# Paired input tiles, the first stage of batch 1 held in SBUF, and one first-stage tile earlier, in a Fourier layer ahead of two feed-forward layers

## The chip, the cores and the metric

One core of one Trainium2 chip runs the whole program. Times are microseconds (us) on the device. The kernel before took 1247.51 us, the median of three runs (1246.95 to 1249.55). All profiles are of a single execution.

## The reference

The input x has two batches of 3008 positions with 256 channels. A Fourier layer is followed by two feed-forward layers:

```python
X = np.fft.rfft(x, axis=1)                       # along the 3008 positions
Yr = Xr @ w_r - Xi @ w_i + b_r                   # complex 256 x 256 product
Yi = Xr @ w_i + Xi @ w_r + b_i
Yr = np.sign(Yr) * np.maximum(np.abs(Yr) - 0.01, 0.0)    # Yi likewise
y = np.fft.irfft(Yr + 1j * Yi, n=3008, axis=1)
h = y @ w_in                                     # 256 -> 2048
u = (h * np.clip(h + 3.0, 0.0, 6.0) / 6.0) @ w_out       # 2048 -> 256
g = u @ w_gate                                   # 256 -> 1536
out = (g / (1.0 + np.exp(-g)) * (u @ w_val)) @ w_out2    # 1536 -> 256
```

Inputs are float32, except that the weights of the feed-forward layers arrive as 64-bit numbers, which the kernel itself turns into float32.

## The kernel before

**The transform in two stages.** 3008 is 47 x 64, and the transform is done as a Fourier transform of length 47 (first stage), then one of length 64 (second stage). The first stage is a product of a constant 96 x 96 matrix, `fwd1_sb`, with x laid out as 96 rows. Each batch is cut into 8 tiles of 96 x 1024 numbers (384 KB), so there are 16 *first-stage tiles*; tiles 0 to 7 are batch 1, tiles 8 to 15 batch 2. `pre(n)` is one of them: it issues the load of tile n + 3 on SyncE (SP), does two products of 512 columns (the profile counts two passes of TensorE for each float32 product, so 4 in a tile), has ScalarE copy the first half out of PSUM and VectorE the second, into a buffer `bs`, and the store of that buffer to the DRAM scratch `Bd` follows on ScalarE's DMA queue (L252). The buffers `bs` come from a ring of four (tag `bc`, `ring4`), which later serves `cs` too. x has four buffers, two for even and two for odd tiles.

The second stage needs the rows regrouped, so it reads `Bd` back. The 96 rows are 24 groups of 4 rows, and a *quad* is four groups, 16 rows: quad 0 rows 0 to 15, quad 1 rows 16 to 31, up to quad 5. `load_q` (L279) loads a quad's `z` tile, 512 KB, with a run of 1 KB for each row and position; it needs the first stage of the whole batch in DRAM. It also loads that quad's table `m`.

**One quad.** With two batches there are 12 quads in turn, p = 0 to 11. For each of them:
- `s2` (L287), the *second stage*: products of z with m, in two halves of 8 passes. Behind it ScalarE casts the result to a high part, VectorE takes the difference as the low part, and ScalarE writes sign-flipped copies of both, into tiles `xh` and `xl`.
- `ln`, the *complex product* with the 256 x 256 matrices (`linh`, `linl`: `lin` split into a high and a low part by GpSimd in `prepare`), by `mm3` (L113 to L115, three products of parts), in two halves; behind each half VectorE adds the bias and does the soft threshold.
- `ia` (L333), the *inverse* of the second stage, into `cs`, stored to `Cd`. Its last stage, `post`, comes per block of tokens ahead of the feed-forward layer.

**Weights.** `Convert.step()` is one *weight step*: it advances the conversion of the first feed-forward layer's weights (64 pieces of 128 x 256) by one piece. In a step VectorE has four instructions (shift L161, tail L165, sign L174, low L181), ScalarE two (scale L156, high L177), and SP one load of 256 KB. Steps are issued by the first-stage tiles above 8, by `ln`, and by the *units* of the feed-forward layer (one unit is one block of tokens with one of 16 slices of the hidden width).

**The order.** All is written out by hand, in one list `seq`, in which each engine finds its own instructions in order; nothing is moved by a scheduler. The list begins with tile 0, `prepare`, tiles 1 to 7, `load_q` of quad 0, tiles 8 to 10 and the second stage of quad 0. Then each turn p brings the first half of quad p's product, half of the inverse of quad p - 1, a first-stage tile, the second stage of quad p + 1, the second half of the product, another tile, and the rest of the inverse, with two tiles a turn until all 16 are used:

```python
seq = P[:1] + [prepare] + P[1:NT] + [lambda: load_q(0, 0)] + P[NT : NT + 3] + S(0)
rest = P[NT + 3 :]
for p in range(len(ORDER)):
    l, a = L(p), A(p - 1)
    some, rest = rest[:2], rest[2:]
    seq += [l[0], a[0]] + u + some[:1] + S(p + 1)[:1] + u + S(p + 1)[1:] + [l[1]] + u + some[1:] + [a[1]] + u
```

`S(p + 1)` begins with the load of quad p + 2. Before any of this, TensorE runs three *warm-up* products on a tile of zeros (L225). Each engine's DMA issues take their semaphores from a few that come round in turn, so an issue can wait for the earlier DMA that had the same one.

## Time and profile before

| | before |
|---|---|
| time, median of 3 (range) | 1247.51 us (1246.95 to 1249.55) |
| profiled execution: time, span of its trace | 1247.67 us, 1245.9 us |
| TensorE (PE) busy, share of the span | 1228.3 us, 99% |
| TensorE weight loads (PEld) | 1034.2 us, 83% |
| VectorE (DVE) | 809.8 us, 65% |
| ScalarE (ACT) | 679.7 us, 55% |
| GpSimd (POOL) | 6.3 us, 1% |
| HBM read, written | 132.75 MB, 39.06 MB |

The span is the stretch from the first to the last instruction in the trace; the time of the execution has 1.8 us more around it. The products of TensorE follow one another without gaps nearly everywhere: in 40 slices of 31 us the profile shows it at 70% in the first, 80% in the second and 90% or more from there on, all but the last. The same first slices have the DMA engines at 90% and 90%, then 70%, 60%, 30%, and the granted TensorE clock at 90% and 80% of full speed, and at 90% or more afterwards.

### The profile page before, as it was taken

To read this page: it belongs to the slowest core of one execution; us is meant where nothing else is said; L and a number is where in the kernel's file an instruction comes from. 1 tells how busy PE (TensorE), PEld (TensorE's weight loads), DVE (VectorE), ACT (ScalarE), POOL (GpSimd) and SP (SyncE) were. 2 spreads that over 40 slices of the span, in tenths; PEclk is the share of its full clock that TensorE was granted. 3 is DMA by queue.
4 is the path that set the end of the run, shared out by engine and by line. 5 is a ranking of instruction groups with operands and counts; after the bars stand their busy time and mean duration, and the time that the engine had idled before them with its cause. 6 is when DMAs were issued, how large, how long until landed. Compare 5 with 4: busy or idle time off the path is not lost.

```text
span 1245.9 us, 15942 instructions
## 1 busy us (share of the span) xinstructions
PE 1228.3 (99%) x5914; PEld 1034.2 (83%) x5914; DVE 809.8 (65%) x1424; ACT 679.7 (55%) x1216; POOL 6.3 (1%) x15
## 2 busy tenths in 40 slices
PE   7899999999999999999999999999999999999998
PEld 2799987888888888888899888888888888888997
DVE  2587665666666666666656577676676676676665
ACT  2455544555555555555555566656656555656554
POOL 2000000000000000000000000000000000000000
PEclk9899999999999999999999999999999999999999
DMA  9976323033122122132032244554644644544551
GB/s 305 279 258 191 102 77 105 28 100 103 64 91 93 59 70 93 64 100 91 39 105 91 72 175 170 203 182 152 220 158 170 235 153 152 216 157 168 203 186 72
DMA packets 50285, 172.84 MB, mean 139 GB/s; under 512 B 4752, under 2 KB 18160, under 8 KB 39456
## 3 DMA queue, kind: packets, MB, share of 16 engines
q1 hardware_dynamic: 41856, 158.55, 37.4%
q10 hardware_dynamic: 8128, 12.58, 2.8%
q8 instruction: 46, 0.75, 0.2%
q0 software_dynamic: 224, 0.69, 0.2%
q14 instruction: 31, 0.25, 0.1%
HBM read 132.75 MB, written 39.06 MB: 138 GB/s over the span
## 4 chain that ended last, share of the span: by engine, by line
PE 96%; DMA 2%; DVE 0%; ACT 0%; issue 0%; SPq 0%; ACTq 0%; DVEq 0%
PE acc L114 12%; PE acc L115 12%; PE acc L113 12%; PE ph L113 7%; PE ph L115 7%; PE ph L114 7%; PE P L662 5%; PE P L663 5%; PE P L664 5%; PE Tb L663 3%; PE Tb L662 3%; PE Tb L664 3%; PE p L419 3%; PE p L113 2%; PE p L115 2%; PE p L114 2%
## 5 line engine op out<-in xcount | busy, mean ns | idle before, releaser
L434 DVE SCALAR_TENSOR_TENSOR r<-r,ph 128x512 f32<-128x512 f32 (+1 forms) x192 | 129.7, 676 | 83.3 <-ACT r L433 82.8
L118 DVE TENSOR_TENSOR gl<-r,gh 128x512 fp32r<-128x512 f32 (+1 forms) x192 | 130.1, 678 | 82.4 <-ACT gh L452 81.0
L433 ACT ACTIVATE r<-ph,three 128x512 f32<-128x512 f32 (+1 forms) x192 | 130.2, 678 | 96.1 <-PE ph L115 80.6
L452 ACT CAST gh<-r 128x512 fp32r<-128x512 f32 (+1 forms) x192 | 117.3, 611 | 84.4 <-DVE r L434 82.7
L113 PE MATMUL ph<-xah,w1l 128*128 128x512 f32 (+1 forms) x384 | 152.1, 396 | 0.0
L113 PE MATMUL acc<-gh,w1l 128*128 128x512 f32 (+1 forms) x384 | 148.3, 386 | 1.5 <-ACT gh L452 1.5
L114 PE MATMUL acc<-gl,w1h 128*128 128x512 f32 (+1 forms) x384 | 148.2, 386 | 0.2 <-DVE gl L118 0.2
L115 PE MATMUL ph<-xah,w1h 128*128 128x512 f32 (+1 forms) x384 | 148.2, 386 | 0.0
L114 PE MATMUL ph<-xal,w1h 128*128 128x512 f32 (+1 forms) x384 | 148.1, 386 | 0.0
L115 PE MATMUL acc<-gh,w1h 128*128 128x512 f32 (+1 forms) x384 | 148.1, 386 | 0.0
L118 DVE TENSOR_TENSOR gl<-s,gh 128x512 fp32r<-128x512 f32 (+1 forms) x144 | 97.3, 676 | 49.8 <-ACT gh L686 49.7
L662 PE MATMUL P<-xo,slot 128*128 128x512 f32 (+1 forms) x288 | 111.3, 386 | 1.7 <-DVE g L732 0.8
L114 PE MATMUL acc<-gl,slot 128*128 128x512 f32 (+1 forms) x288 | 111.1, 386 | 0.3 <-DVE gl L118 0.2
L113 PE MATMUL acc<-gh,slot 128*128 128x512 f32 (+1 forms) x288 | 111.0, 385 | 0.0
L664 PE MATMUL P<-xo,slot 128*128 128x512 f32 (+1 forms) x288 | 110.9, 385 | 0.0
L115 PE MATMUL acc<-gh,slot 128*128 128x512 f32 (+1 forms) x288 | 110.9, 385 | 0.0
L663 PE MATMUL P<-xo,slot 128*128 128x512 f32 (+1 forms) x288 | 110.9, 385 | 0.0
L728 ACT ACTIVATE s<-g 128x512 f32<-128x512 f32 (+1 forms) x72 | 44.9, 623 | 93.7 <-DVE g L726 93.7
L686 ACT CAST gh<-s 128x512 fp32r<-128x512 f32 (+1 forms) x144 | 88.1, 612 | 1.5 <-DVE s L745 1.2
L113 PEld LDWEIGHTS acc<-gh,w1l 128*128 128x128 f32 x384 | 72.1, 188 | 15.4 <-ACT gh L452 1.9
L114 PEld LDWEIGHTS acc<-gl,w1h 128*128 128x128 f32 x384 | 72.1, 188 | 14.6 <-DVE gl L118 0.9
L115 PEld LDWEIGHTS ph<-xah,w1h 128*128 128x128 f32 x384 | 72.1, 188 | 14.0
(94 smaller groups left out, 2258.7 us busy)
## 6 DMA issues: line engine op xcount, KB each, us to landing
slot<-Wd SPq DMA_DIRECT2D x72, 1152.0 KB, 5.1
st<-in_w SPq DMA_DIRECT2D x68, 256.0 KB, 3.8
Wd<-slot SPq DMA_DIRECT2D x12, 1152.0 KB, 4.7
x<-in_x SPq DMA_DIRECT2D x16, 384.0 KB, 6.5
Bd<-bs ACTq DMA_DIRECT2D x16, 384.0 KB, 5.9
z<-Bd SPq DMA_DIRECT2D x12, 512.0 KB, 6.1
Cd<-cs ACTq DMA_DIRECT2D x12, 512.0 KB, 3.5
Xd<-x SPq DMA_DIRECT2D x20, 256.0 KB, 2.1
```

The costliest lines, as they stand in the source:

```text
L113: nc.tensor.matmul(o, wl, xh, start=start, stop=False)
L114: nc.tensor.matmul(o, wh, xl, start=False, stop=False)
L115: nc.tensor.matmul(o, wh, xh, start=False, stop=stop)
L118: nc.vector.tensor_tensor(out=o, in0=full, in1=hi.bitcast(F32), op=ALU.subtract)
L433: nc.scalar.activation(r[:, :n], p[:, :n], AF.Relu, bias=three)
L434: nc.vector.scalar_tensor_tensor(out=r[:, :n], in0=r[:, :n], scalar=6.0, in1=p[:, :n], op0=ALU.min, op1=ALU.mult)
L452: nc.scalar.copy(hi[:, :n], g[:, :n])
L662: nc.tensor.matmul(o, wl, x[:, 0, :n], start=start, stop=False, skip_group_check=not start)
L663: nc.tensor.matmul(o, wh, x[:, 1, :n], start=False, stop=False, skip_group_check=not start)
L664: nc.tensor.matmul(o, wh, x[:, 0, :n], start=False, stop=True, skip_group_check=not start)
L686: nc.scalar.copy(hi[:, :nb], t[:, :nb])
L728: nc.scalar.activation(s0[:, :n], h, AF.Silu)
```

## The change

**Input.** x lies in DRAM as pairs of tiles, *pair* k being tiles 2k and 2k + 1, with 8 KB for each of the 96 rows. There are four rooms of 128 partitions x 2048; rooms 2 and 3 use the space of the tiles `X` (the former `xh` and `xl`, now one tile). Pair 0 comes as two loads of 96 rows, in partitions 0 to 95. Each later pair comes as two loads, 64 rows into every second partition (0, 2, 4, ...), and 32 rows into every fourth (1, 5, 9, ...); the partitions that no row goes to are set to zero by memsets beforehand, of room 1 by VectorE, of rooms 2 and 3 and the end of room 0 by GpSimd. `fwd1_sb` is 128 x 192: the plain matrix, and one whose rows are spread in the same way. Four pairs are issued at the start and the others after tiles 4, 6, 9 and 11 (`REFILL`).

**First stage.** Batch 1's output goes into one SBUF tile, `stage1`, in space that later holds half of the first layer's weights. Its rows 0 to 31 (the *early rows*, those of quads 0 and 1) are stored by ScalarE after tiles 1, 3, 5, 6 and 7. The other 64 (the *held rows*) are stored by two DMAs of SP, issued behind the load of quad 1's z. Batch 2's output goes into buffers of two tiles, from a *ring of two*, stored once for each two tiles; `cs` uses the same ring, two quads to a buffer.

**Order.** `prepare` stands first, twelve first-stage tiles come ahead of the second stage of quad 0 instead of eleven, tile 12 directly behind it, and one tile follows in turn 0 and two in turn 1. There are two warm-up products instead of three. The first four tiles of batch 2 that had a weight step have none now; the step function is the same, and the steps not yet done are taken up by units 8 to 10 of the feed-forward layer. `inv2` is loaded by SP at turn 6 instead of by GpSimd at the start.

The diff (the parts that only follow a renamed tile are left out):

```diff
-    out = {"fwd1": fwd1, "inv2": fwd1.T, "fwd2": fwd2, "inv1": inv1}
+    both = np.zeros((128, 2 * GW))
+    both[:QP, :GW] = fwd1
+    both[::2, GW:], both[1::4, GW:] = fwd1[:64], fwd1[64:]
+    out = {"fwd1": both, "inv2": fwd1.T, "fwd2": fwd2, "inv1": inv1}
...
-    Bd = [dram.tile([GW, NJ * DIM], F32, name=f"Bd{b}") for b in range(NB)]
+    Bd = [dram.tile([n, NJ * DIM], F32, name=f"Bd{n}") for n in (32, GW - 32, GW)]
...
-    fwd1_sb = misc.tile([QP, GW], F32, name="fwd1_sb")
+    fwd1_sb = misc.tile([128, 2 * GW], F32, name="fwd1_sb")
...
-    def pieces(p, name, src, nf, n, into):
-        out = []
-        for f in range(nf):
-            t = [p.tile([128, n, 256], F32R, name=f"{name}{i}_{f}") for i in "hl"]
-            into[f] = t
-            out += [(src[:, f, j], t[0][:, j], t[1][:, j]) for j in range(n)]
-        return Convert(out)
+    HALF = KF1 // 2
+
+    def weights(f):
+        if f not in W1:
+            t = w1p.tile([128, HALF, 2, 2, 256], F32R, tag=f"w1_{f // HALF}", name=f"w1_{f // HALF}", bufs=1)
+            for i in range(HALF):
+                W1[f - f % HALF + i] = [t[:, i, k] for k in range(2)]
+        return W1[f]
...
-    def ring4(name):
-        return ap_.tile([128, 4 * DIM], F32, tag="bc", name=name, bufs=4)
-
-
     NT = NJ // 4
-    xt = {}
-
-    def load_x(n):
-        b, i = divmod(n, NT)
-        if b < NB:
-            xt[n] = xs_p.tile([128, 4 * DIM], F32, tag="xah" if n % 2 else "xal", name=f"x{b}_{i}", bufs=2)
-            nc.sync.dma_start(xt[n][:QP], x[b][:, i * 4 * DIM : (i + 1) * 4 * DIM])
+    TC = 4 * DIM
+    room, bs = {}, {}
+
+    def load_x(k):
+        t, src = room[k], x[k * 2 // NT, k % (NT // 2)]
+        if k == 0:
+            for n in range(2):
+                nc.sync.dma_start(t[:QP, n * TC : (n + 1) * TC], src[:, n * TC : (n + 1) * TC])
+        else:
+            nc.sync.dma_start(t[::2], src[:64])
+            nc.sync.dma_start(t[1::4], src[64:])
     nc.sync.dma_start(fwd1_sb, fwd1)
-    for n in range(3):
-        load_x(n)
+    for k in range(4):
+        if k < 2:
+            room[k] = xs_p.tile([128, 2 * TC], F32, tag="xa", name=f"room{k}", bufs=2)
+        else:
+            room[k] = ap_.tile([128, 3 * TC], F32, tag="X", name=f"room{k}", bufs=2)[:, : 2 * TC]
+        for h in range(2 if k else 0):
+            (nc.vector if k == 1 else nc.gpsimd).memset(room[k][:, h * TC : (h + 1) * TC], 0.0)
+        load_x(k)
+    nc.gpsimd.memset(room[0][96:], 0.0)
+    for k in range(4, NB * NT // 2):
+        room[k] = room[k % 2]
     p = psf[0]([128, 512], "p0")
-    for n in range(3):
+    for n in range(2):
         nc.tensor.matmul(p, zeros[:, :128], zeros, start=True, stop=True)
-    conv1 = pieces(w1p, "w1", w1, KF1, 2, W1)
+    conv1 = Convert([w1[:, f, j] for f in range(KF1) for j in range(2)])
...
         nc.gpsimd.dma_start(bias_sb, bias)
-        nc.gpsimd.dma_start(inv2_sb, inv2)
         for dh in range(2):
...
+    EARLY = 32
+    stage1 = w1p.tile([128, NT * TC], F32, tag="w1_1", name="stage1", bufs=1)
+
     def pre(n):
+        sent()
         b, i = divmod(n, NT)
-        load_x(n + 3)
-        bs = ring4(f"bs{b}_{i}")
+        if b == 0:
+            o = stage1[:GW, i * TC : (i + 1) * TC]
+        else:
+            if n % 2 == 0:
+                bs[n // 2] = ap_.tile([128, 2 * TC], F32, tag="bc", name=f"bs{n}", bufs=2)
+            o = bs[n // 2][:GW, n % 2 * TC : (n % 2 + 1) * TC]
         for h in range(2):
             p = psf[0]([GW, 512], f"p1_{b}_{i}_{h}")
-            nc.tensor.matmul(p, fwd1_sb, xt[n][:QP, h * 512 : (h + 1) * 512], start=True, stop=True)
-            o = bs[:GW, h * 512 : (h + 1) * 512]
+            rhs = room[n // 2][:, (2 * (n % 2) + h) * 512 : (2 * (n % 2) + h + 1) * 512]
+            if n < 2:
+                nc.tensor.matmul(p, fwd1_sb[:QP, :GW], rhs[:QP], start=True, stop=True)
+            else:
+                nc.tensor.matmul(p, fwd1_sb[:, GW:], rhs, start=True, stop=True)
             if h == 0:
-                nc.scalar.copy(o, p)
+                nc.scalar.copy(o[:, :512], p)
             else:
-                nc.vector.tensor_copy(o, p)
-        sent()
-        out_b.append(lambda: nc.scalar.dma_start(Bd[b][:, i * 4 * DIM : (i + 1) * 4 * DIM], bs[:GW]))
-        if i == NT - 1:
-            sent()
+                nc.vector.tensor_copy(o[:, 512:], p)
+        if b == 0 and (i % 2 or i == NT - 2):
+            c = slice((i - (i < NT - 2)) * TC, (i + 1) * TC)
+            out_b.append(lambda: nc.scalar.dma_start(Bd[0][:, c], stage1[:EARLY, c]))
+            if i == NT - 1:
+                sent()
+        elif n % 2:
+            out_b.append(lambda: nc.scalar.dma_start(Bd[2][:, (i - 1) * TC : (i + 1) * TC], bs[n // 2][:GW]))
+            if i == NT - 1:
+                sent()
+        if n in REFILL:
+            load_x(REFILL[n])
+
+    REFILL = {4: 4, 6: 5, 9: 6, 11: 7}
+
+    def rest_of_stage1():
+        for c in (slice(0, NT * TC // 2), slice(NT * TC // 2, NT * TC)):
+            nc.sync.dma_start(Bd[1][:, c], stage1[EARLY:GW, c])
...
         z_t[b, Q] = ap_.tile([128, 4, DIM], F32, tag="z", name=f"z{b}_{Q}", bufs=3)
-        nc.sync.dma_start(z_t[b, Q], bview[b][:, Q * 4 : Q * 4 + 4, :])
+        k, at = (2, Q) if b else (0, Q) if Q < 2 else (1, Q - 2)
+        nc.sync.dma_start(z_t[b, Q], bview[k][:, at * 4 : at * 4 + 4, :])
...
         if dh == 0:
-            X[b, Q] = [ap_.tile([128, 2, 4, 3 * K2], F32R, tag=f"x{k}", name=f"x{k}_{b}_{Q}", bufs=2) for k in "hl"]
+            t = ap_.tile([128, 2, 2, 4, 3 * K2], F32R, tag="X", name=f"X{b}_{Q}", bufs=2)
+            X[b, Q] = [t[:, k] for k in range(2)]
         p = psf[0]([128, 4, 128], f"p2_{b}_{Q}_{dh}")
...
     def ia(b, Q, h):
-        if h == 0:
-            cs[b, Q] = ring4(f"cs{b}_{Q}").rearrange("r (g d) -> r g d", g=4)
+        if h == 0 and Q % 2 == 0:
+            t = ap_.tile([128, 2, 4, DIM], F32, tag="bc", name=f"cs{b}_{Q}", bufs=2)
+            for i in range(2):
+                cs[b, Q + i] = t[:, i]
         p = psf[0]([128, 2, DIM], f"p5_{b}_{Q}_{h}")
...
         pre(n)
-        if n > NT:
+        if n > NT + 4:
             conv1.step()
     P = [lambda n=n: pre_conv(n) for n in range(NB * NT)]
-    seq = P[:1] + [prepare] + P[1:NT] + [lambda: load_q(0, 0)] + P[NT : NT + 3] + S(0)
-    rest = P[NT + 3 :]
+    seq = [prepare] + P[:NT] + [lambda: load_q(0, 0)] + P[NT : NT + 2] + [lambda: load_q(0, 1), rest_of_stage1]
+    seq += P[NT + 2 : NT + 4] + S(0) + P[NT + 4 : NT + 5]
+    rest = P[NT + 5 :]
     for p in range(len(ORDER)):
         l, a = L(p), A(p - 1)
-        some, rest = rest[:2], rest[2:]
+        some = [rest.pop(0) for i in range(1 if p == 0 else 2) if rest]
         u = [lambda: unit()] if p >= FROM else []
...
         if p == NQ:
-            seq += [lambda: load_ct(blocks[0])]
+            seq += [lambda: nc.sync.dma_start(inv2_sb, inv2), lambda: load_ct(blocks[0])]
         if p == FROM - 1:
...
-    xp = np.pad(xp, ((0, 0), (0, QP - QN), (0, 0)))
+    xp = np.pad(xp, ((0, 0), (0, QP - QN), (0, 0))).reshape(NB, QP, NJ // 8, 8 * DIM).transpose(0, 2, 1, 3)
```

On SP, which issues the loads, this is the stretch around quad 0's z before (`x_i_...` is batch 2's tile i, that is tile 8 + i, `m` and `z` the table and tile of a quad, `st` weights):

```order
L217 DMA x_1_221<-in_x 96x1024
L217 DMA x_2_231<-in_x 96x1024
L270 DMA m_242<-in_fwd 128x512
L279 DMA z_0_244<-Bd_60 128x4x256
L217 DMA x_3_246<-in_x 96x1024
L217 DMA x_4_255<-in_x 96x1024
L151 DMA st<-in_w 128x256
L217 DMA x_5_267<-in_x 96x1024
L151 DMA st<-in_w 128x256
L270 DMA m_279<-in_fwd 128x512
L279 DMA z_1_281<-Bd_60 128x4x256
```

And this is the same stretch now; a room is loaded by two DMAs:

```order
L222 DMA room_112<-in_x 64x2048
L223 DMA room_112<-in_x 32x2048
L308 DMA m_200<-in_fwd 128x512
L318 DMA z_0_202<-Bd_60 128x4x256
L222 DMA room_109<-in_x 64x2048
L223 DMA room_109<-in_x 32x2048
L308 DMA m_219<-in_fwd 128x512
L318 DMA z_1_221<-Bd_60 128x4x256
L292 DMA Bd_61<-stage_131 64x4096 x2
L222 DMA room_112<-in_x 64x2048
```

z of quad 1 stands ahead of the load of pair 7 (the last row) and of the held rows' store (`Bd<-stage`), where before three tiles of x, two pieces of weights and a table stood between the two z.

On TensorE, this is the start of quad 0 before (`p_1_i_h` is half h of batch 2's tile i; `p_0_0_0` and `p_0_0_1` the halves of quad 0):

```order
L245 MATMUL p_1_2_0_270<-x_2_231,fwd_sb 96x512
L245 MATMUL p_1_2_1_273<-x_2_231,fwd_sb 96x512
L287 MATMUL p_0_0_0_285<-m_242,z_0_244 128x128 x4
L287 MATMUL p_0_0_1_294<-m_242,z_0_244 128x128 x4
L113 MATMUL p_0_0_0_309<-linh,xl_0_284 128x256
L114 MATMUL p_0_0_0_309<-linl,xh_0_283 128x256
```

And now:

```order
L271 MATMUL p_1_2_1_230<-room_112,fwd_sb 96x512
L271 MATMUL p_1_3_0_233<-room_112,fwd_sb 96x512
L271 MATMUL p_1_3_1_236<-room_112,fwd_sb 96x512
L327 MATMUL p_0_0_0_242<-m_200,z_0_202 128x128 x4
L327 MATMUL p_0_0_1_251<-m_200,z_0_202 128x128 x4
L271 MATMUL p_1_4_0_262<-room_109,fwd_sb 96x512
L271 MATMUL p_1_4_1_265<-room_109,fwd_sb 96x512
L116 MATMUL p_0_0_0_272<-linh,X_0_241 128x256
L117 MATMUL p_0_0_0_272<-linl,X_0_241 128x256
```

Tile 11 (`p_1_3`) now runs ahead of quad 0's second stage, and tile 12 (`p_1_4`) between it and the product, where the product followed the second stage directly.

On ScalarE, this is the end of turn 1 before, from a copy of quad 0's inverse to the casts of quad 2's second stage (`head` and `w1h` belong to a weight step):

```order
L334 COPY cs_0_482<-p_0_0_0_483 128x512
L248 COPY bs_5_487<-p_1_5_0_488 96x512
L252 DMA Bd_61<-bs_4_422 96x1024
L177 CAST w1h_120<-wt 128x256
L156 ACTIVATE head<-st 128x256
L291 CAST xh_2_509<-p_0_2_0_511 128x4x128
L292 ACTIVATE xh_2_509<-p_0_2_0_511 128x4x64
```

And now:

```order
L376 COPY cs_0_409<-p_0_0_0_410 128x512
L282 DMA Bd_62<-bs_261 96x2048
L273 COPY bs_415<-p_1_6_0_416 96x512
L159 ACTIVATE head<-st 128x256
L331 CAST X_2_434<-p_0_2_0_435 128x4x128
L332 ACTIVATE X_2_434<-p_0_2_0_435 128x4x64
```

The store in the second row was of tile 12 alone, into its own buffer of four, with tile 13's copy ahead of it; now it is of tiles 12 and 13 together, and tile 14's copy (the third row) writes into the buffer that this store reads.

## Rows read from the trace of the kernel before

**Rows 1.** TensorE's waits, whole run: us in total, times, longest.

```profile
PE p L287 <- DMA z<-Bd: 6.4, 1, 6.4
PE p L245 <- DMA x<-in_x: 1.6, 3, 0.7
```

**Rows 2.** Windows of 10 us: busy us by engine, granted clock, DMA share, GB/s.

```profile
10.00:20.00 10.00, 9.88 (x24) 3.42 (x23) 3.94 (x6) 3.32 (x6) 2.71 (x5) 1.00 1.02 346
20.00:30.00 10.00, 7.12 (x16) 2.04 (x14) 2.93 (x5) 2.32 (x4) 0.00 (x0) 1.00 1.01 357
30.00:40.00 10.00, 5.35 (x22) 4.85 (x22) 1.38 (x2) 2.08 (x6) 0.00 (x0) 0.66 1.00 263
```

**Rows 3.** ScalarE's DMA queue (packets, MB, share), 10:30, then 30:40 us.

```profile
q10 hardware_dynamic: 1105, 3.90, 52.2%
...
q10 hardware_dynamic: 15, 0.03, 0.8%
```

**Rows 4.** TensorE's timeline: start, duration, line, operation, passes.

```profile
1.48 4.80 PE L225 MATMUL p<-zeros 128*128 128x512 f32 x6 [1.48 <-DVE zeros L127]
6.12 1.88 PE L245 MATMUL p<-x,fwd_sb 96*96 96x512 f32 x4
...
24.23 3.75 PE L245 MATMUL p<-x,fwd_sb 96*96 96x512 f32 x8 [0.61 <-DMA x<-in_x]
34.33 3.75 PE L287 MATMUL p<-m,z 128*128 128x128 f32 x16 [6.35 <-DMA z<-Bd]
...
42.40 1.88 PE L245 MATMUL p<-x,fwd_sb 96*96 96x512 f32 x4
44.12 1.95 PE L287 MATMUL p<-m,z 128*128 128x128 f32 x16
...
48.78 1.88 PE L245 MATMUL p<-x,fwd_sb 96*96 96x512 f32 x4
...
55.96 1.95 PE L287 MATMUL p<-m,z 128*128 128x128 f32 x16
```

**Rows 5.** Timeline of VectorE at 21 us and SP at 28 us.

```profile
21.54 0.69 DVE L250 COPY bs<-p 96x512 f32<-96x512 f32 x1 [1.36 <-PE p L245]
...
28.45 0.40 SPq L279 DMA_DIRECT2D z<-Bd  x1
```

**Rows 6.** Single DMA issues, at 1, 22, 135, 209 us; slot of all.

```profile
x<-in_x SPq DMA_DIRECT2D x1, 384.0 KB, 4.0
...
Bd<-bs ACTq DMA_DIRECT2D x1, 384.0 KB, 6.0
...
z<-Bd SPq DMA_DIRECT2D x1, 512.0 KB, 3.7
...
Xd<-x SPq DMA_DIRECT2D x2, 256.0 KB, 2.0
...
slot<-Wd SPq DMA_DIRECT2D x72, 1152.0 KB, 5.1
```

**Rows 7.** Timeline of VectorE at 1 us and GpSimd at 8 us.

```profile
0.94 0.48 DVE L127 MEMSET zeros<- 128x512 f32 x1
...
8.24 0.40 POOL L236 CAST linh<-lin_st 128x256 fp32r<-128x256 f32 x1 [5.25 <-DMA lin_st<-in_lin]
```

**Rows 8.** ScalarE's timeline, quad 1's casts, first and last.

```profile
45.22 0.58 ACT L291 CAST xh<-p 128x512 fp32r<-128x512 f32 x1 [0.83 <-PE p L287]
...
48.78 0.42 ACT L294 ACTIVATE xl<-xl 128x256 fp32r<-128x256 f32 x1 [0.76 <-DVE xl L118]
```

**Rows 9.** VectorE's groups, 44 to 200 us: busy, mean ns, idle.

```profile
L165 DVE SCALAR_TENSOR_TENSOR wt<-st,wt 128x256 uint32<-128x256 uint32 x32 | 13.3, 417 | 0.0
...
L161 DVE TENSOR_SCALAR wt<-head 128x256 uint32<-128x256 uint32 x32 | 9.1, 285 | 0.0
```

**Rows 10.** Windows of 20 us in the feed-forward start.

```profile
160.00:180.00 20.00, 20.00 (x133) 18.29 (x132) 13.10 (x25) 9.34 (x21) 0.00 (x0) 1.00 0.17 53
180.00:200.00 20.00, 20.00 (x113) 17.58 (x112) 18.14 (x44) 10.69 (x25) 0.00 (x0) 1.00 0.17 54
```

More of the change, by code (lines that the diff above doesn't have):

```diff
@@ L150, in load @@
             t = wst.tile([128, 256], I64, tag="st", name="st", bufs=4)
-            nc.sync.dma_start(t, self.pieces[i][0])
+            nc.sync.dma_start(t, self.pieces[i])
             self.st[i] = t.bitcast(U32).rearrange("p (n t) -> p n t", t=2)
@@ L176, in high @@
         def high(self, i):
-            nc.scalar.copy(self.pieces[i][1], self.full[i])
+            f, j = divmod(i, 2)
+            nc.scalar.copy(weights(f)[0][:, j], self.full[i])
         def low(self, i):
-            _, hi, lo = self.pieces[i]
+            f, j = divmod(i, 2)
+            hi, lo = (t[:, j] for t in weights(f))
             nc.vector.tensor_tensor(out=lo, in0=self.full.pop(i), in1=hi.bitcast(F32), op=ALU.subtract)
@@ L398, in pair @@
     def pair(p, tag):
-        return [p.tile([128, 2, BLK], F32R, tag=f"{tag}{i}", name=f"{tag}{i}", bufs=2) for i in "hl"]
+        t = p.tile([128, 2, 2, BLK], F32R, tag=tag, name=tag, bufs=2)
+        return [t[:, k] for k in range(2)]
     def load_ct(k):
@@ L562, in steps @@
                 yield
-    conv2 = Convert2([(w2[:, f, j], None, None) for f in range(KF2) for j in range(3)])
+    conv2 = Convert2([w2[:, f, j] for f in range(KF2) for j in range(3)])
     steps = conv2.steps()
```

## Prediction

> **What bounds the kernel now.** I read the waits of TensorE first, then the windows of the first 50 us, then TensorE's timeline there, then single transfers. TensorE is busy in 1228.3 of 1245.9 us, and the waits say where the rest is: one wait of 6.4 us for the first z tile, three of 1.6 us in all for x tiles [rows 1]. After that it hardly stops, so the time is the moment at which TensorE becomes gapless plus the work that is then left. The windows show why it is late: from 10 to 40 us the 16 DMA engines are fully busy (1.00 to 1.02), moving 346, 357 and then only 263 GB/s, and the granted clock of 30 to 40 us is 0.66, a mean of the two levels [rows 2]. The queues tell the two rates apart: from 10 to 30 us ScalarE's stores are 52.2% of the DMA time, from 30 to 40 us 0.8% [rows 3]; loads by themselves are slower here than loads beside stores. The timeline gives the steps [rows 4]. First-stage tiles run from 6.12 us, 11 of them (batch 1 whole, three of batch 2) done at 27.98; a tile costs 1.72 us (from 42.40 to 44.12), so 18.9 us of the 21.9 are work. The second stage starts at 34.33, after 6.35 idle. Its 16 passes take 3.75 us there and 1.95 us at 44.12 and 55.96; the complex product behind it takes 4.3 us (38.08 to 42.40) and the next one 2.7 (46.07 to 48.78). [...]
>
> **The change part by part.** The yardstick is the start of quad 2's second stage, 55.96 us before. Between the first second-stage pass and it stands the same list in both kernels (two second stages, three products, one inverse, three tiles): 21.63 us before, 18.5 without the clock loss. Only the tile numbers differ: 11 to 13 before, 12 to 14 now, so one tile less, 1.72 us, is left behind it.
>
> *First stage.* One warm-up product less (2 of 6 passes, 4.80 us for six) frees TensorE at about 4.9 us. The first x tile landed 4.0 us after its issue, at 5.2, beside lin's 0.66 MB [rows 6], which now goes out only behind GpSimd's memsets; fwd1 grows from 0.04 to 0.10 MB ahead of it. I take 5.0 (4.9 to 5.8, if the first tile still runs at the lower level). Eight tiles end at 18.8, twelve at 25.7, if x keeps up.
>
> *Memsets.* VectorE's two of 128x1024 cost twice 0.96 (0.48 for 512 [rows 7]): pair 1 is issued at 3.5, needed at 8.4. GpSimd's are not in the trace; by VectorE's row 1.0, by its own cast (0.40 for 256 columns) 1.6 each, so six memsets' worth end at 6.4 to 10.0. Pair 2 then goes out at 4 and is needed at 11.9, pair 4 at 10.0 and is needed at 18.8. I cost them at nothing; the tiles in front hide them. At 3 us each the cover would be gone: pair 4 at 18.4, tile 8 waiting 3.6. lin's split on GpSimd ends near 20 and is needed at 30.
>
> *The early rows.* Before, the last store of batch 1 went out at 22.3, took 6.0 us in the crowd [rows 6], and z was issued at 28.45 [rows 5]. Now the last store is 0.13 MB, issued 0.8 us after tile 7 (a VectorE copy of 0.69 [rows 5]): 19.6. It takes 2.0 (a 256 KB store alone [rows 6]) to 6.0; I take 2.5, as only 0.13 MB of it remain and SP's loads thin out while they wait for their turn. z is issued at 22.1. It takes 3.7 alone, 5.9 before (28.45 to 34.33): I take 3.9. The second stage starts at 26.0 instead of 34.33, gain **8.3**, behind twelve tiles instead of eleven, gain **1.7**, and 0.3 us of idleness leaves the clock up, gain **3.1** (it stayed at 1.00 through the waits of up to 0.7 us before 28 us [rows 1, 2] and fell in the 6.35). The rows 0 to 31 are one block of partitions. [...]
>
> *What is late next: pair 6.* Tile 12 now stands between the second stage and the product. Its pair can only be issued after tile 9 (22.2), behind z in SP's queue and beside batch 2's first store (0.79 MB each). z, pair and store are 2.1 MB. At 350 GB/s (the windows of 10 to 30 us) they take 6.0 us; with about 2 us around a transfer (z's 3.7 alone, less 1.5 for its 0.52 MB) pair 6 lands at 30.1, TensorE is there at 27.9: cost **2.2** (0 if the store comes behind, 4.2 at 263 GB/s). Quad 2 would start at 30.1 + 16.5 = 46.6.
>
> *The other rows.* Quad 2's z needs the 64 held rows (2.1 MB), which SP issues only behind the first batch-2 store, since a DMA semaphore comes round again. Up to this z the DMA engines carry 14.9 MB: 6.8 before the first z (x 4.7, lin 0.66, early rows 1.05, tables) and 8.1 from it on (z 1.57, pairs 1.57, batch-2 stores 1.57, held rows 2.1, tables and weights 1.3). That is 42.6 us at 350, from 2.4 us on, plus 2 for the last landing: 47.0. Cost **0.4** over the 46.6. The 350 holds where half is stores, as from 22 us on (3.7 of 8.1 MB); in the first 22 us it is nearly all loads. There I count on the spread rows: a load of 1152 KB into all 128 partitions takes 5.1 us [rows 6], 3.1 without the 2 around it, 380 GB/s, so loads alone can be that fast. With 263 there it is rival A.
>
> *The ring of two.* Tile 14's output takes the buffer of tiles 12 and 13, whose store ScalarE issues right in front of tile 14's copy. That copy waits a whole transfer (0.79 MB: 4.2 us alone, about 6 in the crowd), from about 45 to 51, and behind it on ScalarE and VectorE stand quad 2's casts. From the first cast to the last sign flip is 4.0 us (45.22 to 49.20 [rows 8]), 5.0 with the copy and a weight step. The product needs them at 54.5, its second half 0.7 later: cost **0.3** (0 to 3).
>
> *Weight conversion.* Four steps move from the first-stage tiles to units 8 to 10 of the feed-forward layer. A step is four VectorE instructions (one of 0.28, three like that of 0.42 [rows 9]), 1.5 us, so 6.1 us fall into a stretch like 160 to 180 us, where VectorE is busy 13.1 of 20. From 180 to 200 it was busy 18.1 and TensorE never stopped [rows 10]. I take **0.3** (0 to 6.1). The cs pairs find their buffers free, stored a whole quad earlier, and inv2's load on SP has two quads (over 20 us) until its use; both 0.
>
> Sum: 8.3 + 1.7 + 3.1 - 2.2 - 0.4 - 0.3 - 0.3 = 9.9 us. The profiled execution took 1247.67 (span 1245.9), so 1237.8; it lies 0.16 over the median, 1247.51. Predicted: **1237.6 us**.
>
> **The rivals.** *A, the spread loads are no faster than the old ones.* Then the 6.8 MB ahead of the first z go at 263 (25.9 us) and the 8.1 behind it at 350 (23.1): quad 2 at 2.4 + 25.9 + 23.1 + 2 = 53.4, gain 4.3, less the 0.6 of ring and conversion, **1244.0**. For it: the 263 of 30 to 40 us. Against it: the 380 of a 128-partition load. [...] No run here shows a spread load.
>
> *B, slower than before.* If the small stores and the strided loads hold all of it down, the place is the wait for quad 2's z, and the price 4.4 + 14.9 / rate. It decides from 57.7 us (55.96 + 1.72), 280 GB/s over the whole stretch; below it the kernel is slower. At 263: 61.1, a loss of 3.4, with the 0.6 **1251.7**. For it: that row exists. Against it: it had 0.8% stores.
>
> *C, no change*: the same place at 275 to 290 GB/s, **1247**.
>
> *D, VectorE overflows* in units 8 to 11: at worst the whole 6.1 us of the four steps reach TensorE, **1243.5**. For it: 13.1 + 6.1 of 20. Against it: the 18.1 of 20 that cost nothing.
>
> **How the numbers follow.** Forecast (330 to 400 GB/s) 0.60, its own range 1235.0 to 1240.5; A 0.17; D 0.06; C 0.07; B 0.06; 0.04 for a still better one (no wait for pair 6 and z: 1235.2). The range 1234.5 to 1244.2 holds the forecast, D and most of A. A measurement tells 0.2% (2.5 us) from no change: under 1245.0 is faster, 0.86; 1245.0 to 1250.0 the same, 0.08; above, slower, 0.06.
>
> **What would show it.** Right: the first second-stage pass at 25.5 to 27 with under 1 us idle before it and a granted clock of 1.00 from 30 to 40 us; tile 12's matmul with 1 to 3 us of wait for the pair-6 load; quad 2 at 46 to 48; DMA at 340 GB/s or more from 10 to 45 us; a ScalarE copy of about 5 us wait on the store of tiles 12 and 13. Wrong: a wait for an x pair before tile 7 (memsets or slow spread loads), a second wait above 3 us at quad 2 (A, B), TensorE gaps on gl or w1 between 140 and 190 us (D), or first-stage passes at the lower clock level beyond the second tile.

## The result and the profile after

| | before | after |
|---|---|---|
| median (range) | 1247.23 us (1246.78 to 1249.55), 4 runs | 1260.73 us (1258.44 to 1261.72), 4 runs |
| ratio, 95% interval | | 1.0102 (1.0082 to 1.0121) |
| profiled execution: time, span | 1247.67, 1245.9 us | 1261.72, 1259.9 us |
| TensorE busy | 1228.3 us | 1243.8 us |

The change makes the kernel 13.5 us slower; 1237.6 was forecast, and the range ended at 1244.2. A few executions of the runs below took 2.5 to 6 times as long (3191 us in a first run with 256 bytes, E8, which has no other; 7078 us in the traced one of E3); the comparisons leave them out, and no reading rests on their traces.

TensorE's waits after the change (us in total, times, longest), the lines that answer to [rows 1]:

```profile
PE p L327 <- DMA z<-Bd: 4.8, 1, 4.8
PE p L116 <- DVE X L121: 1.6, 3, 0.9
...
PE p L269 <- DMA room<-in_x: 0.3, 1, 0.3
```

The wait for z has gone from 6.4 to 4.8 us, that for x from 1.6 to 0.3, and that for VectorE in the complex product has grown from 0.3 to 1.6. So TensorE waits less, and is busy 15.5 us more. The windows that answer to [rows 2] (busy us by engine, granted clock, DMA share, GB/s):

```profile
10.00:20.00 10.00, 10.00 (x24) 3.78 (x23) 3.43 (x5) 3.06 (x6) 4.31 (x8) 1.00 0.83 284
20.00:30.00 10.00, 8.96 (x21) 3.10 (x19) 4.12 (x6) 3.33 (x6) 0.00 (x0) 1.00 0.74 222
30.00:40.00 10.00, 6.29 (x26) 4.98 (x27) 1.78 (x3) 2.54 (x7) 0.00 (x0) 0.66 1.00 380
```

The DMA engines are no longer full before 30 us, and from 30 to 40 us TensorE still has 0.66 of its clock. TensorE's timeline (start, duration, line, operation, passes), for [rows 4]:

```profile
1.49 3.78 PE L240 MATMUL p<-zeros 128*128 128x512 f32 x4 [1.49 <-DVE zeros L130]
5.53 6.26 PE L269 MATMUL p<-room,fwd_sb 96*96 96x512 f32 x8 [0.26 <-DMA room<-in_x]
11.62 17.33 PE L271 MATMUL p<-room,fwd_sb 128*96 128x512 f32 x40
33.71 3.76 PE L327 MATMUL p<-m,z 128*128 128x128 f32 x16 [4.75 <-DMA z<-Bd]
...
54.11 1.95 PE L327 MATMUL p<-m,z 128*128 128x128 f32 x16
...
66.95 1.95 PE L327 MATMUL p<-m,z 128*128 128x128 f32 x16
...
76.98 2.00 PE L327 MATMUL p<-m,z 128*128 128x128 f32 x16
```

The second stage of quad 0 starts at 33.71, not at 26.0, that of quad 2 at 54.11 (55.96 before, with one tile more to come). Three more rows of the kernel before, the second stages of quads 3 and 4 and the first product of the second feed-forward layer:

```profile
68.65 1.95 PE L287 MATMUL p<-m,z 128*128 128x128 f32 x16
...
77.92 1.95 PE L287 MATMUL p<-m,z 128*128 128x128 f32 x16
...
709.81 0.47 PE L662 MATMUL P<-xo,slot 128*128 128x512 f32 x1 [0.76 <-ACT x L442]
```

and the last of these after:

```profile
718.48 0.47 PE L706 MATMUL P<-xo,slot 128*128 128x512 f32 x1 [0.76 <-ACT x L486]
```

Quad 3, behind which no first-stage tile is left in either kernel, is 1.70 us ahead (66.95 against 68.65), quad 4 0.94 (76.98 against 77.92). At the second layer the kernel is 8.67 us **behind** (718.48 against 709.81), and by the span 14.0. The loss lies in the feed-forward layers, where no wait of TensorE has grown. The second layer takes the blocks in six *pairs*, 0 to 5. Windows of 50 us before, one in the first layer and two in the second (pairs 1 and 2); behind each busy time the number of instructions stands in brackets:

```profile
300.00:350.00 50.00, 50.00 (x236) 41.94 (x235) 31.92 (x62) 26.16 (x44) 0.00 (x0) 1.00 0.22 70
800.00:850.00 50.00, 50.00 (x223) 41.39 (x222) 35.93 (x56) 30.25 (x53) 0.00 (x0) 1.00 0.55 203
900.00:950.00 50.00, 50.00 (x223) 41.39 (x222) 36.03 (x56) 29.33 (x52) 0.00 (x0) 1.00 0.47 167
```

and after:

```profile
300.00:350.00 50.00, 50.00 (x230) 40.83 (x230) 30.58 (x58) 26.20 (x44) 0.00 (x0) 1.00 0.24 75
800.00:850.00 50.00, 50.00 (x218) 40.56 (x217) 34.68 (x55) 29.34 (x51) 0.00 (x0) 1.00 0.58 208
900.00:950.00 50.00, 50.00 (x222) 41.38 (x221) 35.55 (x56) 30.35 (x53) 0.00 (x0) 1.00 0.56 206
```

TensorE is busy throughout and the granted clock is 1.00 in all six, yet it gets through 230 passes instead of 236 in the first layer and 218 instead of 223 in the first window of the second, and through 222 instead of 223 in the last. From start to start (the *pitch*) a pass of 512 columns takes 227 ns before; after the change it takes 224 to 241, on average 233 in the first layer and 232 in pairs 1 and 3 of the second. Pairs 0, 2 and 4 keep 227.

Passes of 448 columns, which the last two blocks of the first layer and pair 5 have, hardly change: 206 ns from start to start before and 204 after in the first layer, 203 and 203 in pair 5. A group of them in the first layer, from 640 to 705 us, before and after (the last number but one is the mean duration in ns):

```profile
L115 PE MATMUL ph<-xah,w1h 128*128 128x448 f32 x52 | 19.1, 368 | 0.0
```

```profile
L118 PE MATMUL ph<-xa,w 128*128 128x448 f32 x51 | 18.7, 366 | 0.0
```

### The profile page after: what moved, and what is told of

It is laid out like the page before. It is cut to its first block, busy times and chain, and to the rows that moved or that the text cites. A ratio compares the mean times of both kernels' runs of the same rounds, so it can differ in the third digit from the quotient of the medians.

```text
span 1259.9 us, 15918 instructions
## 1 busy us (share of the span) xinstructions
PE 1243.8 (99%) x5912; PEld 1035.0 (82%) x5912; DVE 811.4 (64%) x1426; ACT 679.1 (54%) x1216; POOL 11.1 (1%) x19
## 4 chain that ended last, share of the span: by engine, by line
PE 95%; DMA 2%; ACT 1%; DVE 1%; issue 0%; ACTq 0%; SPq 0%; DVEq 0%
PE acc L117 12%; PE acc L118 12%; PE acc L116 12%; PE ph L116 7%; PE ph L118 7%; PE ph L117 7%; PE P L706 5%; PE P L707 5%; PE P L708 5%; PE Tb L708 3%; PE Tb L707 3%; PE Tb L706 3%; PE p L463 3%; PE p L116 2%; PE p L117 2%; PE p L118 2%
## 5 line engine op out<-in xcount | busy, mean ns | idle before, releaser
L116 PE MATMUL ph<-xa,w 128*128 128x512 f32 (+1 forms) x384 | 153.4, 400 | 0.0
L116 PE MATMUL acc<-gh,w 128*128 128x512 f32 (+1 forms) x384 | 149.8, 390 | 1.2 <-ACT gh L496 1.2
L117 PE MATMUL acc<-gl,w 128*128 128x512 f32 (+1 forms) x384 | 149.9, 390 | 0.3 <-DVE gl L121 0.2
L118 PE MATMUL ph<-xa,w 128*128 128x512 f32 (+1 forms) x384 | 149.8, 390 | 0.0
L117 PE MATMUL ph<-xa,w 128*128 128x512 f32 (+1 forms) x384 | 149.7, 390 | 0.0
L118 PE MATMUL acc<-gh,w 128*128 128x512 f32 (+1 forms) x384 | 149.7, 390 | 0.0
L116 PEld LDWEIGHTS acc<-gh,w 128*128 128x128 f32 x384 | 72.2, 188 | 16.8 <-ACT gh L496 1.6
L117 PEld LDWEIGHTS acc<-gl,w 128*128 128x128 f32 x384 | 72.2, 188 | 16.2 <-DVE gl L121 1.0
L118 PEld LDWEIGHTS acc<-gh,w 128*128 128x128 f32 x384 | 72.2, 188 | 15.3
```

The lines of the kernel that those rows point to most:

```text
L116: nc.tensor.matmul(o, wl, xh, start=start, stop=False)
L117: nc.tensor.matmul(o, wh, xl, start=False, stop=False)
L118: nc.tensor.matmul(o, wh, xh, start=False, stop=stop)
```

## The experiments

**Which part makes the passes longer?** No instruction of the feed-forward layers was edited, but places in SBUF were moved. Tiles are laid out from the left and from the right end. `fwd1_sb`, at the left end, grew from 384 to 768 bytes a partition, and all left tiles behind it moved by 384: `xa`, `gh`, `gl`, `slot`, `raw` and the even pairs' `xo`. `w1` and the odd pairs' `xo` come from the right and stayed. TensorE streams one tile while it takes weights from another (from 300 to 350 us before, weight loads run in 41.94 of the 50 us in which it is busy with passes). In the first layer these come from the two sides, in the second layer in the odd pairs only (pair 5 among them, but with 448 columns). In the even pairs VectorE and ScalarE use tiles of the right while TensorE reads the left alone, and a pass keeps its 227 ns; of the passes of 512 columns only those of the first layer (233) and of pairs 1 and 3 (232) are slow, and there TensorE's own two tiles lie on two sides. Before, both sides began at multiples of 512 bytes (`xal` at 26624, `w1h_0` at 163328); after, `xa` is at 27008. That is theory P, the rival is M (merged tiles).

E1 moves the left by 128 bytes more, to 512 in all:

```diff
     inv2_sb = misc.tile([GW, QP], F32, name="inv2_sb")
+    misc.tile([128, 32], F32, name="pad")
```

> The changed kernel with 128 unused bytes a partition behind inv2_sb, so that all tiles of the left side of SBUF (fwd1_sb grew by 384 bytes there) lie 512 bytes from where they lay before the change. Nothing else differs. Theory P (the place in SBUF of the tiles on the left against those on the right lengthens TensorE's passes): the pitch of 512-column passes in both feed-forward layers goes back from 232 to 227 ns, the mean of a pass of the first layer from 395 to 390 ns, and the 14.2 us that the layers lost (9.5 and 4.75) come back: 1246.5 us (1245 to 1248). Rival M (the merged tiles of the high and low parts, or another part of the change, lengthen the passes): pitch stays at 232, 1260.7 us.

E2 moves the right instead (`EDGE = 480` to `608`, the size of an unused tile there):

> The changed kernel with the unused tile at the right end of SBUF 128 bytes larger (480 to 608), so that the tiles on the right move by 128 bytes and those on the left stay where the change put them. Theory P in its relative form (what counts is the distance between the tile that streams and the tile that the weights come from, modulo 512 bytes or less): the distance is again a multiple of 512, pitch 227 ns, 1246.5 us (1245 to 1248). Theory P in its absolute form (the tiles on the left lie badly by themselves): pitch stays at 232 ns where the streaming tile is on the left, 1260 us. Rival M: 1260.7.

E3 moves the left of the kernel *before* by 384 bytes and does nothing else:

> The kernel before, with 384 unused bytes a partition behind inv2_sb and no other edit: the tiles on the left move by what the change moved them. Theory P: 512-column passes go from 227 to 232 ns in the first feed-forward layer and in two of the six pairs of blocks of the second, 1247.2 + 14.2 = 1261.4 us (1259 to 1263). Rival M: unchanged, 1247.2 us.

Measured: E1 1246.17 us, ratio to before 0.9980 (0.9969 to 0.9991); E2 1246.67, 0.9985 (0.9974 to 0.9997); E3 1261.72, 1.0103 (1.0078 to 1.0127). Theory P holds in its relative form, M falls. The address of the left tiles in itself does not matter, since E2 leaves them where the change put them and only the right follows. E2's first window:

```profile
300.00:350.00 50.00, 50.00 (x236) 41.95 (x235) 32.05 (x62) 26.02 (x45) 0.00 (x0) 1.00 0.22 69
```

236 passes, as before the change. 384 unused bytes alone cost the old kernel 13.4 us (1261.72 against 1248.3 in the same runs); E3 speaks by its time alone, and the passes are counted in the run of 128 bytes below.

**What distance is free?** Three more paddings of the kernel before: 128, 256 and 64 bytes.

> The kernel before with 128 unused bytes on the left side, no other edit. If only multiples of 512 are free of the slowdown, pitch about 232 ns and 1260 us, as at 384; if the distance acts by its sign or by its size, something between 227 and 232 ns; if 128 is a multiple of the period, 227 ns and 1247.5 us (then 384 would not be slow, so this is the least likely).

> The kernel before with 256 unused bytes on the left side, no other edit. If the distance between the streaming tile and the weights counts modulo 512, pitch of the passes that read from both sides about 232 ns, 1260 us; if modulo 256 or less, 227 ns and 1247.5 us.

> The kernel before with 64 unused bytes on the left side, no other edit. At 0, 256 and 512 bytes of difference the passes had 227 ns, at 128 and 384 232 ns. If only multiples of 256 are free, 64 is slow too: about 232 ns, 1260 us. If what counts is an odd multiple of 128 alone, 227 ns and 1247.3 us; if the price grows with the distance from a multiple of 256, about half: 1254 us.

The results, with 384 and 512 from above:

| left moved against right, bytes | time | ratio (95%) |
|---|---|---|
| 64 | 1254.11 us | 1.0053 (1.0035 to 1.0072) |
| 128 | 1261.01 us | 1.0106 (1.0084 to 1.0128) |
| 256 | 1247.50 us | 0.9998 (0.9988 to 1.0009) |
| 384 (E3) | 1261.72 us | 1.0103 (1.0078 to 1.0127) |
| 512 (E1, with the change) | 1246.17 us | 0.9980 (0.9969 to 0.9991) |

The windows at 128 bytes:

```profile
300.00:350.00 50.00, 50.00 (x231) 40.96 (x231) 30.93 (x58) 25.96 (x44) 0.00 (x0) 1.00 0.25 75
800.00:850.00 50.00, 50.00 (x218) 40.56 (x217) 34.56 (x54) 29.31 (x52) 0.00 (x0) 1.00 0.57 206
```

at 256:

```profile
300.00:350.00 50.00, 50.00 (x237) 41.93 (x236) 31.78 (x62) 26.32 (x44) 0.00 (x0) 1.00 0.23 71
```

and at 64:

```profile
300.00:350.00 50.00, 50.00 (x234) 41.55 (x233) 31.27 (x59) 26.37 (x44) 0.00 (x0) 1.00 0.23 73
800.00:850.00 50.00, 50.00 (x217) 40.33 (x216) 35.14 (x55) 29.87 (x52) 0.00 (x0) 1.00 0.58 208
```

128 alone gives the picture of the change; 256 is free; 64 costs about half in the first layer (234 passes) and all of it in pair 1. So the free distances for passes of 512 columns are, of those tried, the multiples of 256. For 448 columns no distance costs as much: in the first layer such a pass takes 206 ns from start to start at 0 and 256 bytes, 204 at 128 and 384, and 200 at 64. Why the number of columns matters was not tried.

**The start (E4).** In the timeline after, six of the eight passes of tiles 0 and 1 ran at half speed: 6.26 us for eight, where a tile of four takes 1.72. E4 is E1 with the third warm-up product:

```diff
-    for n in range(2):
+    for n in range(3):
         nc.tensor.matmul(p, zeros[:, :128], zeros, start=True, stop=True)
```

> The changed kernel with the 128 bytes of the run before and the third warm-up product back. Theory W (the warm-up product that was taken out kept TensorE busy until the first x tile came, and without it 6 passes more ran at the lower clock level): warm-up ends at about 6 us, tile 0 runs at once at the higher level, tile 7 ends 2.0 to 2.6 us earlier than 22.07, z of quad 0 is issued that much earlier than 26.13 and the second stage of quad 0 starts at about 31 instead of 33.7; if nothing later takes it back, 1.5 to 2.6 us less than without the third product, about 1244.3. Rival (the loads of x set the pace): TensorE waits for x pairs between tiles 2 and 7, z is issued at about 26, the same time as without.

1245.69 us, 0.9982 (0.9968 to 0.9996). Its timeline:

```profile
1.49 5.34 PE L241 MATMUL p<-zeros 128*128 128x512 f32 x6 [1.49 <-DVE zeros L131]
6.67 3.60 PE L270 MATMUL p<-room,fwd_sb 96*96 96x512 f32 x8
...
27.69 2.02 PE L328 MATMUL p<-m,z 128*128 128x128 f32 x16 [0.26 <-DMA z<-Bd]
32.71 2.57 PE L272 MATMUL p<-room,fwd_sb 128*96 128x512 f32 x4 [3.00 <-DMA room<-in_x]
```

Tiles 0 and 1 take 3.60 us for eight passes, as theory W had it. But E1, with two warm-up products, does so too:

```profile
5.74 3.64 PE L270 MATMUL p<-room,fwd_sb 96*96 96x512 f32 x8 [0.46 <-DMA room<-in_x]
...
32.14 3.75 PE L328 MATMUL p<-m,z 128*128 128x128 f32 x16 [4.82 <-DMA z<-Bd]
```

and E2, with two as well, takes 3.68 us behind a wait of 1.02. So theory W is not borne out: with the same two products the level was up at tile 0 in two traces and came up only at 10.7 us in the third, the one after the change, and tile 7 ends at 19.7 us in E1, at 20.6 in E4. The times agree with that: E4 hardly gained on E1, where 1244.3 was expected.

What E4's trace has beside E1's is a faster way to z. Its last early store took 2.0 us instead of 4.1, and z 4.2 instead of 7.4, so that quad 0's second stage starts at 27.69 with 0.26 us of wait. Then the forecast's next wait appears, 3.00 us at tile 12 for pair 6 (2.2 forecast), and the clock falls behind it (0.83 from 30 to 40 us), so that quad 2 starts at 50.75. Single runs of E4 lie between 1243.2 and 1249.0; what differs among them one trace cannot say. E4's z, issued at 23.39 us, 1.4 ahead of the first store of batch 2 (the last column is the time to landing):

```profile
z<-Bd SPq DMA_DIRECT2D x1, 512.0 KB, 4.2
```

and z after the change, issued at 26.13, 0.2 ahead of that store:

```profile
z<-Bd SPq DMA_DIRECT2D x1, 512.0 KB, 7.4
```

**The ring of two (E5).** ScalarE around tile 14's copy, after the change:

```profile
52.65 0.31 ACTq L282 DMA_DIRECT2D Bd<-bs  x1
59.35 0.58 ACT L273 COPY bs<-p 96x512 f32<-96x512 f32 x1 [6.17 <-DMA Bd<-bs]
```

The store of tiles 12 and 13 goes out at 52.65, a turn after tile 13, and the copy behind it waits 6.17 us. From quad 2's second stage to quad 3's it takes 12.84 us, where 12.69 less a tile (1.72) would be 10.97. E5 is E4 with

```diff
             out_b.append(lambda: nc.scalar.dma_start(Bd[2][:, (i - 1) * TC : (i + 1) * TC], bs[n // 2][:GW]))
-            if i == NT - 1:
+            if i == NT - 1 or n == 13:
                 sent()
```

> The kernel with 128 bytes and three warm-up products (the run before), and the store of tiles 12 and 13 issued right behind tile 13's copies instead of in front of tile 14's copy, a turn later. Theory R (the ring of two: tile 14's copy waits 6.4 us on ScalarE and 6.0 on VectorE for a store that was issued just in front of it, and quad 2's casts stand behind it): the copy finds its buffer free at 50 us, quad 2's product starts without the 0.5 and 0.86 us of waits, the stretch from quad 2's to quad 3's second stage goes from 14.6 us to 11 to 12, and the time falls by 2.5 to 3.5 us: about 1242.7 us. Rival (the stretch is long because of z, x or weights that land late): it stays at 14 us or more with a DMA wait of TensorE, 1245.7 us.

1243.58 us, 0.9966 (0.9952 to 0.9981). The second stages of quads 2 and 3:

```profile
52.88 1.95 PE L328 MATMUL p<-m,z 128*128 128x128 f32 x16
...
63.86 1.95 PE L328 MATMUL p<-m,z 128*128 128x128 f32 x16
```

10.98 us, where E4 has 14.56, so theory R holds; the time fell by about 2 us, less than expected, and the intervals of the two ratios overlap. Quad 2 itself was late this time (52.88): z of quad 0, issued at 24.91 just behind the store of batch 2 (24.50), took 7.8 us.

**Tile 12 later (E6).** E5 with two tiles in turn 0, as before the change:

```diff
-    seq += P[NT + 2 : NT + 4] + S(0) + P[NT + 4 : NT + 5]
-    rest = P[NT + 5 :]
+    seq += P[NT + 2 : NT + 4] + S(0)
+    rest = P[NT + 4 :]
```

> The run with the store behind tile 13, and tile 12 behind the first half of quad 0's product instead of directly behind quad 0's second stage (two tiles in turn 0 as before the change). Theory T (the 3.0 us wait for pair 6 is in the place of tile 12 alone): the wait goes, the clock stays at its higher level, quad 2's second stage comes 3 to 4 us earlier, at about 47, and the time falls by 3: about 1239.7. Rival D (the DMA engines set the pace up to quad 2's z, which landed at 49.6 because the held rows are stored late): the wait for pair 6 goes but one of 2 to 4 us stands in front of quad 2's second stage instead, which starts at about 50; the time stays within 1 us of the run before, 1242.7.

1244.92 us, 0.9977 (0.9964 to 0.9989): no gain over E5, as rival D had it, but not by its mechanism. z of quad 0 took 7.0 us again, beside the store, so that pair 6 was not waited for in any case, and quad 2 started at 52.41. The loss is behind it. ScalarE, from the store of tiles 12 and 13 to quad 2's first cast:

```profile
47.99 0.31 ACTq L283 DMA_DIRECT2D Bd<-bs  x1
...
52.97 0.44 ACT L160 ACTIVATE head<-st 128x256 f32<-128x256 f32 x1 [4.19 <-DMA st<-in_w]
...
58.25 0.43 ACT L160 ACTIVATE head<-st 128x256 f32<-128x256 f32 x1 [3.75 <-DMA st<-in_w]
58.59 0.57 ACT L332 CAST X<-p 128x512 fp32r<-128x512 f32 x1
```

Two weight steps wait 4.19 and 3.75 us for their pieces in front of the casts. SP issued the second only at 53.85, as the store of 47.99 landed. Whether pair 6's wait can be hidden in this way is not settled.

**Which transfers slow z (E10, E12).** In six traces so far (after, E1, E2, E5, E6, E7) z took 6.6 to 8.4 us, with the first store of batch 2 issued between 0.6 us ahead of it and 0.3 behind; in E4, with the store 1.4 behind, 4.2. E10 and E12 are E5 with that store later:

```diff
     def pre(n):
-        sent()
+        if n != 10:        # E10; in E12: if n not in (10, 11), and sent() behind tile 11
+            sent()
```

> The kernel with 128 bytes, three warm-up products and the store behind tile 13, and the first store of batch 2 (tiles 8 and 9, 0.79 MB on ScalarE's queue) issued in front of tile 11's copies instead of tile 10's, 1.7 us later. Theory C (quad 0's z takes 4.2 us where that store is issued 1.4 us behind it, as in the run with three warm-ups alone, and 7.0 to 8 us where it is issued with it or ahead of it, as in all the others): the store goes out at about 26, z of quad 0 takes 4 to 5 us, the second stage starts at 27.5 to 29.5, tile 12 may wait up to 3 us for pair 6, quad 2 starts at or before 50.5 and the time is 1 to 2.5 us under the 1243.6 of the run before, about 1241.8. Rival (pair 6 or the DMA engines as a whole slow z): z still takes 7 us, second stage at 32 to 33, 1243.6.

> The kernel with 128 bytes, three warm-up products and the store behind tile 13, and both first stores of batch 2 (tiles 8, 9 and 10, 11) issued behind tile 11's copies, 2 us later than in the run before. Theory C (quad 0's z takes about 4 us where no store of batch 2 is issued within a microsecond of it, 7 to 8 where one is): stores go out at 27.5 to 28.5, z of quad 0, issued at 23.4 to 25.4, takes 3.7 to 4.8 us, the second stage starts at 27.7 to 30.2. What is late next is tile 12, whose pair and whose buffer (the store of tiles 8 and 9) come at about 33, and quad 2's z at about 50: quad 2's second stage at 50 to 52.5, time 1242 to 1243.5. Rival (the loads of pair 6 behind z on the same queue slow z): z takes 7 us again, the second stage starts at 32 to 33, 1243.5.

E10: 1243.36 us, 0.9965 (0.9951 to 0.9978), inconclusive by its trace: the early rows landed only at 25.41, so z went out with the store after all (25.43 and 25.41) and took 6.9 us, a seventh slow one beside the store. E12: 1242.56 us, 0.9962 (0.9949 to 0.9976), the lowest median, though its interval does not set it apart from E5 and E10. Its z, issued at 24.35, the first store at 26.57:

```profile
z<-Bd SPq DMA_DIRECT2D x1, 512.0 KB, 3.8
```

though pair 6's loads were issued 0.5 and 1.0 us behind z. So pair 6 on the same queue does no harm (3.8 us), the store on ScalarE's queue does (6.6 to 8.4); theory C holds. TensorE:

```profile
28.25 2.02 PE L329 MATMUL p<-m,z 128*128 128x128 f32 x16 [0.95 <-DMA z<-Bd]
31.97 1.93 PE L273 MATMUL p<-room,fwd_sb 128*96 128x512 f32 x4 [1.69 <-DMA room<-in_x]
...
48.41 1.13 PE L377 MATMUL p<-yp,n 128*128 128x256 f32 x4 [2.41 <-DMA n<-in_inv]
...
51.72 2.02 PE L329 MATMUL p<-m,z 128*128 128x128 f32 x16 [0.45 <-DMA z<-Bd]
```

Quad 0 starts at 28.25; then every transfer is late by turns: pair 6 (1.69), the table `n` (2.41), z of quad 2 (0.45). E12's windows of 30 to 50 us say why, with the DMA engines full at about 400 GB/s:

```profile
30.00:40.00 10.00, 8.31 (x51) 6.07 (x50) 4.48 (x7) 3.27 (x9) 0.00 (x0) 1.00 1.03 412
40.00:50.00 10.00, 7.59 (x57) 6.97 (x56) 3.58 (x7) 3.08 (x9) 0.00 (x0) 1.00 1.01 395
```

This is the bound that the prediction had put at 47.0 for quad 2's z; it is 51.6. By then 16.5 MB have moved, where 14.9 were counted, and the first 30 us went at 265 GB/s with a DMA share of 0.78, where 350 GB/s was counted from 2.4 us on.

**The spread (E7) and the early rows (E11).** E7 is E4 with the pairs in partitions 0 to 95:

```diff
-            nc.sync.dma_start(t[::2], src[:64])
-            nc.sync.dma_start(t[1::4], src[64:])
+            nc.sync.dma_start(t[:64], src[:64])
+            nc.sync.dma_start(t[64:QP], src[64:])
```

> The kernel with 128 bytes and three warm-up products, and the pairs loaded into 64 and 32 neighbouring partitions (0 to 63, 64 to 95) by two loads of the same sizes, instead of into every second and every fourth partition; the plain matrix for all tiles. Theory S (the spread makes the loads faster, the forecast's ground for 350 GB/s in the first 22 us): x pairs land later, TensorE waits for them between tiles 2 and 11 by 2 us or more in sum, quad 0's second stage starts at 30 or later instead of 27.7. Rival N (HBM or the queues set the pace, not the partitions): no waits for x, second stage at 27.2 to 28.2, the time as without.

1252.65 us (one run). Its wait for x (total, times, longest) and its window of 10 to 20 us:

```profile
PE p L270 <- DMA room<-in_x: 3.6, 3, 2.0
```

```profile
10.00:20.00 10.00, 7.85 (x18) 2.44 (x16) 3.22 (x5) 2.64 (x5) 0.00 (x0) 1.00 1.01 254
```

and that window of E4:

```profile
10.00:20.00 10.00, 10.00 (x25) 3.77 (x24) 4.12 (x6) 2.94 (x6) 4.32 (x8) 1.00 0.88 332
```

254 GB/s with full DMA engines against 332 with a share of 0.88, quad 0 at 37.9 instead of 27.7, 5.9 us of it before z is issued and 4.2 in z, which has the store beside it again: that is theory S, against rival A. Why the choice of partitions matters is not shown.

E11 is E5 with `EARLY = GW`, all 96 rows stored by ScalarE and none held:

> The kernel with 128 bytes, three warm-up products and the store behind tile 13, and all 96 rows of batch 1's first stage stored by ScalarE after the same tiles, none held. Theory E (storing 32 rows first is what brings quad 0's z forward): the last store is 0.39 MB and lands later, z is issued 2 to 4 us later than 24.9, quad 0's second stage starts at 35 or later (32.9 with the early rows) and the time is 1.5 to 4 us higher than 1243.6. Rival (the bytes up to quad 2's z are the same, and with no held rows that z is there early): quad 0 starts later but quad 2 at the same time, the time within 1 us of 1243.6.

1247.73 us, 0.9999 (0.9989 to 1.0009), 4.2 us over E5; quad 0's second stage starts at 35.37. Theory E holds, but most of the delay comes in a way that it did not name, at the x pairs:

```profile
PE p L272 <- DMA room<-in_x: 8.4, 2, 5.5
```

The longer stores of ScalarE hold up the loads: SP waited 7.7 us for one of them and issued pair 4's second load only at 18.67 (16.38 in E4), the load took 7.4 us (2.9 in E4), and TensorE waits 5.5 us for that pair at tile 8 and 2.9 for pair 6 at tile 12. z itself, alone this time, took 3.7 us.

## Why the prediction was wrong, step by step

By the two profiled executions the span grew by 14.0 us, where the forecast had -9.9. Each term, forecast and measured (second stages of quads 0, 2, 3 and 4: S0, S2, S3, S4):

| step | forecast | measured |
|---|---|---|
| S0 earlier | +8.3 | +0.62 (33.71 against 34.33) |
| one tile more done | +1.7 | +1.72 |
| clock kept up, S0 to S2 | +3.1 | +1.23 (20.40 against 21.63) |
| pair 6, then z of quad 2 | -2.6 | 0, no such wait |
| ring of two, S2 to S4 | -0.3 | -2.63 |
| sum at S4 | | +0.94 |
| weight conversion in the first units | -0.3 | no wait in the trace from 100 to 200 us |
| passes of the two layers | not in it | -14.4 (from +0.94 at S4 to -13.4 at the last pass; 0.6 more lies behind it) |

- **The step that decides was not there.** The prediction followed instructions, queues and transfers, and its opening step, that the time is the moment at which TensorE becomes gapless plus the work that is then left, put the passes behind quad 4 at nothing, since no instruction of theirs is edited. That fails: `fwd1_sb` at twice its width is in the diff, and E3 shows that its 384 bytes by themselves cost 13.4 us. None of the rivals held it; that B forecast a slower kernel is luck, since its place, a wait for quad 2's z, is not in the trace. The unused tile of 480 bytes at the right end was the hint: with it both sides begin at multiples of 512.
- **S0 came 7.7 us later than forecast.** Tile 7 ended at 22.1 instead of 18.8: 0.5 because TensorE had x only at 5.5, and 2.6 because six passes ran at the lower level, to 10.7 us (853 ns from start to start, 429 behind them). Those 2.6 belong to this execution: E1 and E2, with the same two warm-up products, do not have them, and there S0 is at 32.14 and 31.71, still some 6 us late. The granted clock reads 1.00 in that stretch, so the level there has to be read from the passes. The last early store took 3.2 us for 2.5 (4.1 in E1), and z 7.4 for 3.9, which by E12 is the store of batch 2 beside it. The prediction had that store beside pair 6 and not beside z.
- **The clock** fell to 0.50 (32 to 38 us) in the wait of 4.75 us, which stayed. In E12 that wait is 0.95 us, the longest one after it up to 60 us 2.41, and the clock is 1.00 from 30 to 50 us, as the step had it. No run shows the step's 3.1 us as one figure; in E12 quad 0's second stage takes 2.02 us and the product behind it, from the end of the passes in front of it, 2.70, where they took 3.75 and 4.32 before, 0.33 of it a wait.
- **Pair 6**: right in mechanism. The wait was hidden by the late S0 and is 3.0 us in E4, 1.7 in E12. The term behind it, quad 2's z, was mis-sized: 51.6 in E12 for 47.0.
- **The ring of two**: right in mechanism, wrong in size and time. The store was taken to be issued at 45, where tile 13 ends; it stands behind the copy of quad 0's inverse and went out at 52.65, so that quad 2's casts came late by it.
- **Memsets and spread loads**: right. No x wait above 0.3 us in this trace; E7, without the spread, is slower (1252.65 us against 1245.69), so rival A falls.

With the addresses put right the change is worth about 2 us (E1, 1246.17 against 1248.3), and with the third warm-up back and three stores moved 4.8 (E12, 1242.56 against 1247.40). No run came near the 9.9: in E12 the DMA engines are full from 30 us on, and quad 2's z lands 4.6 us later than forecast.
